# Retention and two feed-forward layers on one core: a planner that models the shared port, and the attention products by single heads

## The chip, the cores and the metric

The kernel runs on 1 core of one Trainium2 chip. The metric is the device time of one execution in microseconds. The engines are named as in the profile: PE (TensorE, matmuls), DVE (VectorE), ACT (ScalarE), POOL (GpSimd) and SP (SyncE, which issues all DMAs here).

## The reference

Inputs q, k, v are 4 batches x 8 heads x 768 positions x 64; two feed-forward layers have w_in 512 x 2048 and w_out 2048 x 512 each.

```python
gamma = 1.0 - 2.0 ** (-5.0 - np.arange(H))
for t in range(S):
    state = gamma * state + np.einsum('bhd,bhe->bhde', k[:, :, t], v[:, :, t])
    y[:, :, t] = scale * np.einsum('bhd,bhde->bhe', q[:, :, t], state)
x = y.transpose(0, 2, 1, 3).reshape(3072, 512)
h = x @ w_in1;  x = (h * np.cos(h)) @ w_out1
h = x @ w_in2;  out = np.where(h > 0, h, exp(min(h, 0)) - 1) @ w_out2
```

## The kernel before

**Retention in units.** The 768 positions are cut into 6 chunks of 128; a chunk of one batch is a unit n (24 units; c = n // 4 is the chunk, b = n % 4 the batch). Heads go in 4 pairs. A unit is loaded as one tile u of 128 x 2048 floats: q and k by features (512 columns each), then v and k by tokens (512 each). Its steps, with the lines of the functions: `load_unit` (430), `scale_unit` (437: q times its decay and scale, v times gamma to the power -(t+1)), `state_unit` (445: the state times gamma to the 128th, written into the two diagonal blocks of a 128 x 128 matrix per pair, as two operations on 64 partitions, whose other blocks a POOL memset at line 896 has zeroed), `scores` (454: 8 matmuls on halves of the rows, then the causal mask by DVE), `values` (474: for c > 0 four 128 x 128 state products, then 8 products of v with the masked scores; ACT and DVE split the result into a high and a low part, x_t) and `update` (505: four 128 x 128 products of k and v, of which the diagonal blocks are added to the state in two operations; none in the last chunk). A matmul of plain float32 shows as two passes in the profile.

**First layer.** Four units make a block of 512 tokens (6 blocks). `hidden` (545) computes a block's hidden units in 8 steps j of 24 matmuls of 512 columns (high and low parts: three products each), and ACT and DVE apply h cos h. The weights come as 64-bit floats and are converted by ACT and three DVE operations each half (lines 322, 325, 329), then split; in block 0 this is `first_weights`, up to 3 steps ahead. Between the hidden products of block i stand the scores, values and updates of the units of block i + 1. The **front** is the attention of units 0 to 3, before the first hidden product. In it `warm` (884) puts matmuls on zeros between the steps; all write one PSUM tile of pool f.

**Later products** use Strassen-Winograd, 7 products of quarter size. `project` (787) is the output product of a layer, on 3 superblocks of 1024 tokens; `hidden2` (638) is the second layer's hidden product, with `seven`, `elu`, `load_x2`, `differences` around it (`product2`, line 630, has its matmuls).

**Order of work.** Every operation is registered with an engine, an estimated time, what it reads and writes, and tiles of pools w 8, hl 4, ld 3, c 11, h 5, eg 3, f 2 (eg and f are PSUM; f has one bank each). `Plan.run` (140) then simulates the engines on the host and so fixes, once, the order of the instructions on each engine. PE keeps the program's order; DVE, ACT, POOL and SP take the ready operation that is due first. An operation marked ANY (scaling, state, differences, part of the preparation of weights) goes to whichever of DVE and POOL takes it first; its two estimates are for DVE and POOL. Where one of them starts an operation between SBUF operands while the other is in one, the estimate of the one that starts is multiplied by CROWDED = 1.6. An operation with an operand in eg or f doesn't count for this.

## Time and profile before

| | us |
|---|---|
| median of 3 runs | 1118.89 (1115.94 to 1121.49) |
| profiled execution | 1118.94 |
| its span | 1117.2 |
| PE / DVE / ACT / POOL busy | 1077.8 / 857.9 / 620.9 / 411.6 |
| front, to the first hidden product | 33.6 |
| first layer's hidden products, to | 378.5 |
| first output product, to | 607 |
| second hidden layer, to | 868.7 |
| second output product, to the end | 1117.2 |

The busy share of an engine is an average over these stages. A stage is read by its own windows, and PE's loss in it is the difference between its length and its matmuls at the pace of a dense stretch. Times in the rows are microseconds from the start of the span; L290 and L295 are the helpers for ACT and for element-wise operations, so such rows are told apart by tiles.

### The profile page before, as it was taken

How to read it: one execution, taken by the hardware profiler on the slowest of the kernel's cores; microseconds unless marked ns; L12 is line 12 of the kernel's file. 1: busy time of each engine (PE TensorE's matmuls, PEld its weight loads, DVE VectorE, ACT ScalarE, POOL GpSimd, SP SyncE). 2: the span in 40 equal slices, each digit the busy share in tenths (PEclk: the TensorE clock that was granted, in tenths of full speed). 3: DMA queues.
4: the chain of work that ended last, by engine and by line, in shares of the span. 5: the costliest groups of instructions: out<-in, count | busy, mean ns of one | idle time of the engine just before them, and what ended most of it. 6: DMA issues, size and time to landing. Idle time of an engine off the chain costs nothing. (4 is left out here: it accounts for less than half of the span.)

```text
span 1117.2 us, 14628 instructions
## 1 busy us (share of the span) xinstructions
PE 1077.8 (96%) x5382; PEld 880.8 (79%) x5384; DVE 857.9 (77%) x884; ACT 620.9 (56%) x719; POOL 411.6 (37%) x300
## 2 busy tenths in 40 slices
PE   7999999999999999999998999999899999999997
PEld 4788888888888888888886787777687788887886
DVE  6998899888899877556649899887798956565452
ACT  3565455554668753443446677767687744443442
POOL 2223462246445734303204874654453421210000
PEclk8999999999999999999999999999899999999999
DMA  8866898988998899999965657877776999998661
GB/s 314 303 226 231 303 332 320 356 295 315 342 345 290 288 347 329 334 334 352 342 246 171 250 215 289 318 287 279 274 259 232 330 343 328 352 347 281 207 207 57
DMA packets 114695, 323.27 MB, mean 289 GB/s; under 512 B 8640, under 2 KB 14912, under 8 KB 112064
## 3 DMA queue, kind: packets, MB, share of 16 engines
q1 hardware_dynamic: 114624, 322.35, 80.9%
q8 instruction: 42, 0.69, 0.2%
q14 instruction: 29, 0.24, 0.1%
HBM read 195.96 MB, written 126.35 MB: 289 GB/s over the span
## 5 line engine op out<-in xcount | busy, mean ns | idle before, releaser
L826 PE MATMUL eg<-hl,w 128*128 128x512 f32 x2016 | 463.7, 390 | 0.0
L295 POOL TENSOR_TENSOR c<-c 128x512 f32<-128x512 f32 (+2 forms) x207 | 305.3, 1486 | 382.6 <-DMA c<-d 138.1
L826 PEld LDWEIGHTS eg<-hl,w 128*128 128x128 f32 x2016 | 376.9, 188 | 77.7
L295 DVE TENSOR_TENSOR hl<-ld,hl 128x1024 fp32r<-128x1024 f32 x168 | 227.7, 1365 | 110.1 <-ACT hl L290 109.7
L290 ACT ACTIVATE hl<-ld 128x1024 fp32r<-128x1024 f32 x168 | 177.9, 1060 | 230.4 <-PE eg L826 219.2
L290 ACT ACTIVATE c<-c 128x1024 f32<-128x1024 f32 (+1 forms) x256 | 231.3, 920 | 79.3 <-DVE c L574 44.3
L557 PE MATMUL eg<-hl,w 128*128 128x512 f32 x1152 | 273.3, 394 | 0.0
L557 PEld LDWEIGHTS eg<-hl,w 128*128 128x128 f32 x1152 | 213.1, 188 | 49.2 <-issue 2.7
L290 ACT ACTIVATE c<-eg 128x1024 int32<-128x1024 f32 (+2 forms) x96 | 87.6, 912 | 98.4 <-PE eg L557 72.9
L630 PE MATMUL eg<-hl,w 128*128 128x512 f32 x432 | 113.3, 398 | 12.5 <-DVE c L295 11.7
L630 PEld LDWEIGHTS eg<-hl,w 128*128 128x128 f32 x432 | 80.4, 190 | 36.1 <-DVE c L295 18.2
L630 PE MATMUL eg<-ld,w 128*128 128x512 f32 x288 | 76.2, 399 | 8.7 <-DVE ld L295 6.5
L295 DVE TENSOR_TENSOR c<-c 128x512 f32<-128x512 f32 (+2 forms) x61 | 49.5, 813 | 31.7 <-DMA c<-d 24.7
L630 PEld LDWEIGHTS eg<-ld,w 128*128 128x128 f32 x288 | 54.9, 191 | 22.3 <-DVE ld L295 7.5
L295 POOL TENSOR_TENSOR ld<-ld,w 128x512 f32<-128x512 f32 x32 | 44.3, 1397 | 72.1 <-DMA ld<-in_attn 58.8
L383 DVE SCALAR_TENSOR_TENSOR w<-c,w 128x768 fp32r<-128x768 f32 (+1 forms) x48 | 65.7, 1383 | 2.8 <-ACT w L290 2.8
L574 DVE SCALAR_TENSOR_TENSOR c<-eg,c 128x1024 f32<-128x1024 f32 x48 | 58.4, 1217 | 9.9 <-ACT c L290 7.3
L579 DVE SCALAR_TENSOR_TENSOR c<-c,eg 128x1024 f32<-128x1024 f32 x48 | 58.4, 1216 | 8.1 <-ACT c L290 7.3
L295 POOL TENSOR_TENSOR h<-c 128x512 f32<-128x512 f32 x22 | 36.4, 1654 | 60.2 <-DMA d<-h 46.5
L290 ACT ACTIVATE w<-c 128x1024 fp32r<-128x1024 f32 (+3 forms) x59 | 52.8, 920 | 9.8 <-DVE c L329 4.1
L329 DVE SCALAR_TENSOR_TENSOR c<-c 128x512 uint32<-128x512 uint32 x64 | 57.0, 900 | 0.7
L325 DVE SCALAR_TENSOR_TENSOR c<-c 128x512 uint32<-128x512 uint32 x64 | 55.1, 872 | 1.0
(50 smaller groups left out, 792.8 us busy)
## 6 DMA issues: line engine op xcount, KB each, us to landing
d<-c SPq DMA_DIRECT2D x205, 512.0 KB, 4.5
ld<-d SPq DMA_DIRECT2D x84, 1024.0 KB, 7.6
c<-d SPq DMA_DIRECT2D x93, 512.0 KB, 6.0
c<-in_weights SPq DMA_DIRECT2D x64, 512.0 KB, 6.7
ld<-in_attn SPq DMA_DIRECT2D x20, 1024.0 KB, 6.5
d<-h SPq DMA_DIRECT2D x32, 256.0 KB, 8.0
out<-c SPq DMA_DIRECT2D x12, 512.0 KB, 4.5
d<-c SPq DMA_DIRECT2D x16, 256.0 KB, 3.1
```

The lines of the kernel that those rows point to most:

```text
L290: plan.op("ACT", us, lambda: nc.scalar.activation(out=out_(), in_=in_(), func=func, **kw), r, w, lag)
L295: e.tensor_tensor(out=out_(), in0=a(), in1=b(), op=op)
L325: plan.op("DVE", 0.69, lambda: nc.vector.scalar_tensor_tensor(out=u(), in0=raw.t[:, :, 1], scalar=0x80000000, in1=u(), op0=ALU.bitwise_and ...
L329: plan.op("DVE", 0.69, lambda: nc.vector.scalar_tensor_tensor(out=u(), in0=raw.t[:, :, 0], scalar=29, in1=u(), op0=ALU.logical_shift_right ...
L383: plan.op("DVE", 0.08 + 0.29 * (hi - lo), lambda: nc.vector.scalar_tensor_tensor(out=w.t[:, lo:hi, 1, :], in0=view(), scalar=turn, in1=hig ...
L557: nc.tensor.matmul(out=h.t[:, half * TB:(half + 1) * TB], lhsT=quarter(j, qd, wpart, kc % 2), rhs=(xh, xl)[xpart].t[:, kc, :], start=(n == ...
L574: plan.op("DVE", 1.22, lambda: nc.vector.scalar_tensor_tensor(out=g.t, in0=h.t, scalar=1.0 / TWO_PI, in1=n(), op0=ALU.mult, op1=ALU.subtra ...
L579: plan.op("DVE", 1.22, lambda: nc.vector.scalar_tensor_tensor(out=g.t, in0=g.t, scalar=1.0, in1=h.t, op0=ALU.subtract, op1=ALU.mult,), [h, ...
L630: nc.tensor.matmul(out=out_(), lhsT=w.t[:, i, wpart, kc * P:(kc + 1) * P], rhs=x.t[:, xpart, kc, :], start=(start and n == 0), stop=(n == ...
L826: nc.tensor.matmul(out=acc.t[:, i * TB:(i + 1) * TB], lhsT=w[:, A_OF[p], wpart, i * P:(i + 1) * P], rhs=hl.t[:, gpart, k, :], start=(p in ...
```

## The change

The planner: the constant CROWDED goes. While DVE and POOL are both in an operation between SBUF operands, both progress at 0.57 of their rate, recomputed at each start and end. POOL starts nothing while DVE is in such an operation.

The attention: state products and updates go head by head, 8 matmuls of 64 x 64 weights, or of 128 x 64 with 64 moving columns, instead of 4; the state is aged in one operation without zero blocks around it, and added or copied in one. The decay of a position is no longer put on v but, for the scores, into a table `fall` of 8 masks that DVE makes at the start, and for the state on k by tokens, in all but the last chunk. `values` needs only q and v of its unit and no longer the whole tile.

The front: unit 3 is loaded into a tile of pool hl instead of ld. Each `warm` has a PSUM tile of its own, given back after it. The last piece of unit 0 (k by tokens) is loaded ahead of unit 1.

```diff
-CROWDED = 1.6
+SHARED = 0.57
...
+        def pace(now):
+            for eng in ("DVE", "POOL"):
+                if eng in doing:
+                    n, left, since, rate, told = doing[eng]
+                    doing[eng] = [n, left - (now - since) * rate, now, rate, told]
+            both = all(e in doing and port[doing[e][0]] for e in ("DVE", "POOL"))
+            for eng in ("DVE", "POOL"):
+                if eng in doing:
+                    d = doing[eng]
+                    d[3] = SHARED if both else 1.0
+                    end = now + max(d[1], 0.0) / d[3]
...
-                if port[n] and busy[other] > now + 0.1 and on_port[other]:
-                    us *= CROWDED
...
+                if eng == "POOL" and "DVE" in doing and port[doing["DVE"][0]] and busy["DVE"] > now + 0.05:
+                    continue
...
     def scale_unit(n, lag=0):
...
         tt("ANY", (0.65, 1.25), q, q, q_tab, ALU.mult, [u[0, 512], tab_at], [u[0, 512]], lag=lag)
-        tt("ANY", (0.65, 1.25), v, v, lambda: v_tab().to_broadcast([P, H, D]), ALU.mult,
-           [u[1024, 1536], tab_at], [u[1024, 1536]], lag=lag)
+        if n // B < UPB - 1:
+            tt("ANY", (0.65, 1.25), k, k, lambda: s_tab().to_broadcast([P, H, D]), ALU.mult,
+               [u[1536, 2048], tab_at], [u[1536, 2048]], lag=lag)
...
-            for j in range(2):
-                r = slice(j * D, (j + 1) * D)
-                tt("ANY", (0.36, 0.75), lambda r=r: diag(n)[r, :, r], lambda r=r: state(b)[r],
+            tt("ANY", (0.36, 0.75), lambda: aged(n), lambda: state(b), lambda: g_tab().to_broadcast([P, NPAIR, D]),
...
-        tt("DVE", 1.23, flat(pt), flat(sc), mask, ALU.mult, [sc, tab_at], [pt], lag=-80)
+        tt("DVE", 1.23, flat(pt), flat(sc), fall, ALU.mult, [sc, fall_at], [pt], lag=-80)
...
-                for a in range(NPAIR):
+            for a in range(NPAIR if c > 0 else 0):
+                for j in range(2):
+                    r = slice(j * D, (j + 1) * D)
                     nc.tensor.matmul(
-                        out=xps.t[:, a, :], lhsT=diag(n)[:, a, :], rhs=q[:, a, :],
+                        out=xps.t[r, a, :], lhsT=aged(n)[r, a, :], rhs=q[r, a, :],
...
-        plan.op("PE", 1.0 if c == 0 else 1.9, go, [u, pt] + ([diag_at(n)] if c > 0 else []), [xps])
+        need = [u[0, 512], u[1024, 1536], pt] + ([aged_at(n)] if c > 0 else [])
+        plan.op("PE", 1.0 if c == 0 else 1.9, go, need, [xps])
...
-                    out=ds.t[:, a, :], lhsT=u.t[:, 1536 + a * P:1536 + (a + 1) * P],
-                    rhs=u.t[:, 1024 + a * P:1024 + (a + 1) * P], start=True, stop=True,
+                        out=ds.t[j * D:(j + 1) * D, a, :], lhsT=u.t[:, 1536 + h0:1536 + h0 + D],
+                        rhs=u.t[:, 1024 + h0:1024 + h0 + D], start=(a == 0), stop=(a == NPAIR - 1),
...
-        plan.op("PE", 1.0, go, [u[1024, 2048]], [ds])
+        plan.op("PE", 0.55, go, [u[1024, 2048]], [ds])
...
-    rest_ps = Buf("f", [P, TB])
-
     def warm(n):
+        rest_ps = Buf("f", [P, TB])
...
     dma(2, lambda: unit0.t[:, 1024:1536], lambda: attn[0, :, 1024:1536], w=[unit0[1024, 1536]])
-    plan.op("POOL", 1.5, lambda: nc.gpsimd.memset(cst.t[:, DIAG:DIAG + 1024], 0.0), [],
-            [cst[DIAG, DIAG + 1024]])
+    dma(2, lambda: unit0.t[:, 1536:2048], lambda: attn[0, :, 1536:2048], w=[unit0[1536, 2048]])
+    tt("DVE", 1.23, lambda: fall().rearrange("p (j a) t -> p j a t", j=2),
...
-    scale_unit(0, "DVE")
+    scale_unit(0)
...
     load_unit(1, EARLY)
-    dma(2, lambda: unit0.t[:, 1536:2048], lambda: attn[0, :, 1536:2048], w=[unit0[1536, 2048]])
...
-    load_unit(3, EARLY)
+    load_unit(3, EARLY, tag="hl")
```

## Rows read from the trace of the kernel before

**Rows 1.** Windows: stretch, length, busy us (instructions) by engine, granted clock, DMA share, GB/s

```profile
6.18:20.00 13.82, 9.42 (x91) 7.37 (x94) 9.28 (x12) 3.86 (x7) 4.88 (x5) 0.83 0.95 344
20.00:33.63 13.63, 10.21 (x99) 7.26 (x96) 12.96 (x17) 7.26 (x14) 3.88 (x4) 0.92 0.91 337
33.63:60.00 26.37, 26.37 (x162) 22.03 (x161) 25.89 (x34) 15.86 (x20) 8.84 (x8) 1.00 0.77 282
60.00:94.50 34.50, 33.83 (x210) 27.87 (x208) 33.84 (x45) 21.92 (x27) 9.24 (x9) 1.00 0.73 247
94.50:330.00 235.50, 235.50 (x1487) 196.45 (x1486) 207.81 (x249) 124.16 (x141) 104.00 (x89) 1.00 0.88 316
...
378.50:607.00 228.50, 228.50 (x1010) 189.27 (x1009) 158.15 (x121) 110.09 (x108) 67.32 (x33) 1.00 0.86 307
607.00:868.70 261.70, 240.46 (x1011) 190.90 (x1010) 225.74 (x248) 188.49 (x250) 147.62 (x105) 0.97 0.74 268
```

The engines stand in the order PE, PE's weight loads, DVE, ACT, POOL.

**Rows 2.** Windows: two openings of superblocks in the second hidden layer

```profile
607.00:627.20 20.20, 15.05 (x56) 11.01 (x54) 18.25 (x13) 13.06 (x16) 15.80 (x10) 0.83 0.93 322
...
779.60:793.50 13.90, 8.38 (x21) 5.59 (x21) 12.35 (x13) 9.18 (x11) 5.55 (x3) 0.63 0.89 308
```

**Rows 3.** Timeline of the front: start, us, engine, line, operation, tiles, count [idle before, releaser]

```profile
13.56 0.68 DVE L295 TENSOR_TENSOR hl<-f,hl 128x512 fp32r<-128x512 f32 x1
...
14.34 1.22 PE L514 MATMUL f<-ld 128*128 128x128 f32 x8 [1.99 <-issue]
...
15.59 1.28 SPq L287 DMA_DIRECT2D ld<-in_attn  x3
...
21.67 0.68 DVE L295 TENSOR_TENSOR hl<-f,hl 128x512 fp32r<-128x512 f32 x1
...
22.45 1.13 PE L514 MATMUL f<-ld 128*128 128x128 f32 x8 [0.57 <-issue]
...
23.66 0.33 SPq L287 DMA_DIRECT2D ld<-in_attn  x1
...
30.84 1.65 POOL L295 TENSOR_TENSOR ld<-ld,w 128x512 f32<-128x512 f32 x1 [4.73 <-DVE c L329]
...
32.54 1.16 PE L464 MATMUL eg<-ld 64*128 64x128 f32 x16 [1.39 <-POOL ld L295]
```

**Rows 4.** Timeline of PE in the dense stretch: L483 state product, L490 v product, L514 update

```profile
39.21 1.05 PE L483 MATMUL f<-ld,w 128*128 128x128 f32 x8
40.19 1.09 PE L490 MATMUL f<-w,ld 128*64 128x128 f32 x16
41.22 5.74 PE L557 MATMUL eg<-hl,w 128*128 128x512 f32 x24
46.80 1.05 PE L514 MATMUL f<-ld 128*128 128x128 f32 x8
47.78 1.16 PE L464 MATMUL eg<-ld 64*128 64x128 f32 x16
48.87 5.73 PE L557 MATMUL eg<-hl,w 128*128 128x512 f32 x24
...
300.49 5.74 PE L557 MATMUL eg<-hl,w 128*128 128x512 f32 x24
306.16 1.16 PE L464 MATMUL eg<-ld 64*128 64x128 f32 x16
```

L557 is the hidden product and L464 the scores; weights stand as rows * columns, then the moving operand.

**Rows 5.** By line: count, shortest/median/longest ns, first and last start

```profile
L329 DVE SCALAR_TENSOR_TENSOR c<-c x64: 676/689/1784, 16.3 to 825.9; 128x512 uint32<-128x512 uint32 x64
...
L574 DVE SCALAR_TENSOR_TENSOR c<-eg,c x48: 1204/1218/1226, 41.5 to 395.0; 128x1024 f32<-128x1024 f32 x48
```

**Rows 6.** Groups of 607 to 868.7 by shape: count, busy us, mean ns, idle before

```profile
L329 DVE SCALAR_TENSOR_TENSOR c<-c 128x512 uint32<-128x512 uint32 x16 | 15.9, 1007 | 0.1
...
L295 POOL TENSOR_TENSOR c<-c 128x512 f32<-128x512 f32 x58 | 90.8, 1566 | 70.6 <-DVE c L740 26.4 <-DVE c L728 24.0 <-issue 14.7
L295 POOL TENSOR_TENSOR c<-c 128x256 f32<-128x256 f32 x45 | 52.8, 1196 | 31.1 <-DMA d<-c 7.8 <-DVE c L728 7.2 <-DVE w L383 6.0
```

More of the change, by code (lines that the diff above doesn't have):

```diff
@@ L155, in run @@
         port = [op[0] in ("DVE", "POOL", "ANY") and not any(b.tag in ("eg", "f") for b in op[4]) for op in ops]
-        on_port = {"DVE": False, "POOL": False}
         def line(n):
@@ L185, in slot_ok @@
             return True
+        doing = {}
+        def pace(now):
[9 more added lines that the diff above has]
+                    end = now + max(d[1], 0.0) / d[3]
+                    if abs(end - d[4]) > 1e-6:
+                        d[4] = busy[eng] = end
+                        heapq.heappush(events, (end, 0, d[0]))
         def start(n, now, eng):
@@ L191, in start @@
             ran_on[n] = eng
-            if eng in on_port:
-                other = "POOL" if eng == "DVE" else "DVE"
-                on_port[eng] = port[n]
-                if port[n] and busy[other] > now + 0.1 and on_port[other]:
-                    us *= CROWDED
             for buf in news:
@@ L201, in start @@
             fn(eng) if ops[n][0] == "ANY" else fn()
-            busy[eng] = now + us
             work[eng] += us
             log.append((now, eng, n))
+            if eng in ("DVE", "POOL"):
+                doing[eng] = [n, us, now, 1.0, 0.0]
+                pace(now)
+                return
+            busy[eng] = now + us
             heapq.heappush(events, (now + us, 0, n))
@@ L220, in run @@
                 eng = ran_on[n]
+                if eng in ("DVE", "POOL"):
+                    if eng not in doing or doing[eng][0] != n or abs(doing[eng][4] - now) > 1e-6:
+                        continue
+                    del doing[eng]
+                    pace(now)
                 done += 1
@@ L245, in run @@
                     continue
-                lines = [ready[eng], flexible] if eng in on_port else [ready[eng]]
+                if eng == "POOL" and "DVE" in doing and port[doing["DVE"][0]] and busy["DVE"] > now + 0.05:
+                    continue
+                lines = [ready[eng], flexible] if eng in ("DVE", "POOL") else [ready[eng]]
                 back = []
@@ L469, in scores @@
         plan.op("PE", 1.0, go, [u[0, 1024]], [sc])
-        mask = lambda: cst.t[:, 512:640].rearrange("p (o t) -> p o t", o=1).to_broadcast([P, H, P])
         flat = lambda x: (lambda: x.t.rearrange("p j a t -> p (j a) t"))
-        tt("DVE", 1.23, flat(pt), flat(sc), mask, ALU.mult, [sc, tab_at], [pt], lag=-80)
+        tt("DVE", 1.23, flat(pt), flat(sc), fall, ALU.mult, [sc, fall_at], [pt], lag=-80)
     def values(n):
@@ L509, in update @@
             return
[L510 removed]
+        ds = Buf("f", [P, NPAIR, D])
         def go():
             for a in range(NPAIR):
[L514 to L526 removed]
+                for j in range(2):
+                    h0 = (2 * a + j) * D
+                    nc.tensor.matmul(
+                        out=ds.t[j * D:(j + 1) * D, a, :], lhsT=u.t[:, 1536 + h0:1536 + h0 + D],
+                        rhs=u.t[:, 1024 + h0:1024 + h0 + D], start=(a == 0), stop=(a == NPAIR - 1),
+                        skip_group_check=True,
+                    )
+        plan.op("PE", 0.55, go, [u[1024, 2048]], [ds])
+        if c == 0:
+            act(0.4, lambda: state(b), lambda: ds.t, [ds], [state_at(b)], lag=-40)
+        else:
+            tt("DVE", 0.42, lambda: state(b), lambda: ds.t, lambda: aged(n), ALU.add,
+               [ds, aged_at(n)], [state_at(b)], lag=-40)
     gd = {(layer, sb): dram_buf([P, NJ, NP, TB]) for layer in range(2) for sb in range(NSB)}
```

44 lines of the change are left out of this document (19 added, 25 removed).

## The prediction

> **What bounds the kernel now.** I read the stages first [rows 1]. TensorE (PE) is busy 235.50 of 235.50 us from 94.5 to 330 and 228.50 of 228.50 in the first output product, where 1010 matmuls take 0.226 us each. No other engine can shorten those stretches; only fewer or shorter PE passes can. Two stretches are different. Before 33.63 us PE idles (9.42 busy of 13.82, then 10.21 of 13.63). And the second hidden layer, 607 to 868.7, takes 261.70 us for 1011 matmuls that are worth 1011 x 0.226 = 228.7, so it loses 33.0. In [rows 2] 7.5 of these are lost at 607 to 627.2 (20.20 less 56 x 0.226) and 9.2 at 779.6 to 793.5 (13.90 less 21 x 0.226), where a new superblock's inputs are split and the granted clock falls to 0.83 and 0.63 after PE has waited; the other 16.3 are spread.
>
> The third reading is VectorE (DVE) between the front and the end of block 0. It is idle 4.54 us of 6.18 to 20, but only 1.81 us of the 74.5 after that (12.96 + 25.89 + 33.84 busy) [rows 1]. So PE looks dense there while DVE, which converts the weights of block 0, has no room either. Whatever the front gains must pass this gate.
>
> In the timeline of the front [rows 3] the reader is to see PE waiting for a PSUM bank of the pool f: update(0) starts at 14.34, right after DVE's split of x at 13.56 for 0.68 us has ended, and update(1) at 22.45, after the split at 21.67. One of the two f banks is held by the clock-keeping matmuls, so values and update take turns on the other. Unit 3 is asked for at 15.59, when update(0) has freed unit 0's slot, and unit 4 at 23.66, after update(1). Its scaling ends at 30.84 + 1.65, and PE has its first scores at 32.54 after a wait of 1.39.
>
> **The change part by part.** The sum is made against the profiled execution, 1118.94 us (span 1117.2 and 1.7 around it); the median of the runs shown is 1118.89, so nothing is shifted.
>
> Front: f bank, unit 3 in hl, k of unit 0 earlier. update(0) no longer waits 1.99, update(1) 0.57, the first scores 1.39 [rows 3]; the matmuls between them also run at a granted 0.83 and 0.92 [rows 1], so I put PE's possible gain at 4 (those waits) to 8 us. The DVE gate caps it: DVE can take back at most its 4.54 us of idle time, plus the work that leaves it up to the end of block 0. That is one state addition of 0.42 us (the planner's own cost, in the code) per unit instead of two: four units, 1.7 us. Less some 0.6, because the new product of mask and decay (1.23 in the code) stands where unit 0's v was scaled (0.65). So the cap is 4.54 + 1.1 = 5.6. Not every gap can be filled: I take **-4.0**, ends 0 and -5.6. What the moves cost: unit 0's k goes past the three loads of unit 1 on SP, 0.26 MB at 344 GB/s [rows 1], 0.8 us later for unit 1, of which the cap leaves room. New waits: the mask waits for the new table, computed on the same engine ahead of it; update waits for k to be scaled, and behind update on PE the next scores are queued, but between scaling and update lies a whole hidden product of 5.6 us after the front. The POOL memset that goes and the ACT copies of state (8 to 4) lie beside other work: 0, and nothing if that cover is gone, as removed work cannot delay.
>
> State products by heads, in the dense stretch. A block's length is the distance of starts in [rows 4]. The old state product takes 39.21 to 40.19 = 0.98, the old update 46.80 to 47.78 = 0.98, each 8 passes with 128 weight rows, columns and moving columns. The product of v and scores, 16 passes on two column halves with 128 moving columns, takes 1.03; the scores, 16 passes on two row halves, 1.09. The hidden product before a tiled block lasts 5.67 (300.49 to 306.16) where one before a full block lasts 5.58 (41.22 to 46.80): changing over costs 0.09. The new state product has 16 passes on two diagonal quarters with 128 moving columns. No row shows a quarter. Bounds: 1.03 + 0.09 = 1.12 if it goes like the two halves, and 0.52 + 0.09 = 0.61 if smaller weights halve it. The scores have twice the weight columns of the v product and take about as long (1.09 and 1.03), so the moving columns seem to set the pace and these stay: I take 1.12, +0.14. The new update has 64 moving columns, 16 passes. Bounds again 0.61 and 1.12; since the moving columns halve I take half of 1.03 without about 0.15 for starting and ending, 0.15 again, and 0.09, which is 0.68: -0.30. In block 0 the DVE gate rules, so 16 of the 20 state products and 12 of the 20 updates count (four updates lie in the front): 16 x 0.14 - 12 x 0.30 = **-1.4**, ends 28 x 0.14 = +3.9 and 28 x -0.37 = -10.4.
>
> The rows give a block 0.064 us per pass whatever its shape on halves (1.03 over 16) [rows 4], so the number of passes could be the limit instead of the columns; then the update costs 1.12 and PE gains nothing. The Trainium skill, page "TensorE: Matmul & The Clock Gate", section "Wait — 56ns, not 53.3ns?", gives such a rule: with hardware decode off the sequencer spends about 62 ns on each MATMUL. By it the update would take 16 x 0.062 = 0.99, no gain over 0.98; the trace does not contradict it here.
>
> Decay in the mask: v is no longer scaled, k is, with the same shape and as many instructions until the last four units, which drop one each; on POOL these are off the path: 0. One state_unit operation on 128 partitions replaces two on 64; POOL's time, 0.
>
> Port-aware planner. It alters no work, only the order per engine and which of DVE and POOL takes the free operations. Nothing in the trace of before shows the new order, so this is the widest term. What the rows show: a DVE operation with an operand in PSUM is never delayed (L574: 1204 to 1226 ns over 48), one between SBUF operands can be (L329: median 689, up to 1784) [rows 5]. In the second hidden layer the 16 of L329 average 1007, so 0.32 us above the median each, while POOL's 58 operations of 512 columns average 1566 [rows 6]. The old planner counted 1.25 for these and stretched only the later of two that meet; the new one slows both and lets POOL begin when DVE is off the port. An order made from truer lengths should have fewer late arrivals among the 16.3 us spread over this stage, and may do better or worse at the two openings. I take **-3**, about a fifth of 16.3; ends -16 (all spread waits gone) and +12 (the slower rival below). In the output products PE is dense and DVE has 70 us free [rows 1]: there a new order costs 0.
>
> The rows also speak against the planner's model. The longest L329, 1784, is one of 689 plus about 1.1, as if it stood still until a POOL operation had ended, and not run at half speed. The Trainium skill says so: page "SBUF — State Buffer", section "Who interferes with whom": the pair of ports that both engines share is an exclusive lock held for a whole instruction, and the loser waits. By that, a POOL operation that starts in the shadow of a PSUM operation of 0.68 still blocks the next DVE operation, and the planner term would be 0.
>
> Sum: 1118.94 - 4.0 - 1.4 - 3 = 1110.5.
>
> **The rivals.**
> A, given back: the front's gain is eaten at the DVE gate (units 4 to 7 wait for weights), a tile pair costs its 1.12, and the new order is worth nothing: -0.5 to +3.9, about 1119. For it: DVE's 1.81 idle us in 74.5 [rows 1]. Against: 4.54 idle us before them.
> B, slower: DVE takes the free operations that POOL may not begin. In the second hidden layer DVE is busy 225.74 of 261.70 and PE needs 228.7 [rows 1]: DVE has 3 us to spare. An operation of 512 columns moved to DVE adds 0.69 and saves a meeting worth 0.32, net some 0.3 over both sizes. From 10 moved operations on this lengthens the stage. Half of the 103 [rows 6] moved, 52, gives (52 - 10) x 0.3 = 12.6, so 1118.94 - 5.4 + 12.6 = 1126. For it: DVE looks for work at every end, POOL only off the port. Against: three or four PSUM operations a step give POOL its openings.
> C, more: the openings at 607 and 779.6 close too, as their loads and splits come in time: 13 of 16.7 us more, 1097. For it: in both DVE and POOL work side by side. Against: the loads at the openings have little to do with the port.
> That the lock and not the sharing holds is the forecast without the planner's 3: 1113.5, inside the forecast's own spread.
>
> **How the numbers follow.** Forecast (1103 to 1114.5) 0.45, A (1114.5 to 1122) 0.20, B (above 1122) 0.15, C (below 1103) 0.20. Leaving out B and the lower part of C (0.05) gives the range 1095 to 1122, which holds 0.8; it takes in the bounds of the PE term (-10.4, +3.9) around the rest. Half a per cent, 5.6 us, is about what a measurement of this kernel can tell from no change: below 1113.3 lie C and nearly all of the forecast, 0.62; above 1124.5 most of B, 0.13; between them 0.25.
>
> **What would show it.** In the front: update(0) near 12.4 without a wait, unit 3 asked for before 10 us, the first hidden product at 26 to 30 instead of 33.63, and then the gate: PE waits for weights in 45 to 90 and the end of block 0 only about 4 us earlier. Blocks: update 0.6 to 0.75, state product 1.0 to 1.15; 0.5 for both would make the dense stretch 10 us shorter. Second hidden layer: PE's loss below 33, L329's mean below 1007, POOL's count not far under 105. I am wrong if POOL's count halves and DVE is above 230 us there (B), if block 0 ends where it did (A), or if the openings' 16.7 us vanish (C).

## The result, and the profile after

The changed kernel took 1108.38 us in the median (1105.53 to 1110.73, 5 runs); the kernel before took 1117.52 in the runs beside it. The ratio is 0.9916, interval 0.9901 to 0.9931: faster by 0.84%. The forecast was 1110.5, range 1095 to 1122. The profiled execution of the changed kernel took 1108.38 us with a span of 1106.6.

Lines moved: helpers are L314 (ACT) and L319 (element-wise) now, L491 scores, L510 state product, L517 v product, L544 update, L586 first hidden product, L659 second, L855 output products, L353 what L329 was. The kernels of the experiments have line numbers of their own; there rows are told apart by their tiles. First the windows of the changed kernel, cut where the first matmul of each product starts; block 0 ends one matmul (0.23) after the start of its last hidden matmul, and the last output product is counted to the start of its last matmul. The columns are those of [rows 1].

```profile
6.38:26.14 19.76, 15.24 (x220) 11.43 (x221) 16.79 (x22) 7.15 (x13) 8.34 (x7) 1.00 1.02 370
26.14:87.03 60.89, 59.29 (x418) 46.72 (x416) 57.82 (x79) 38.66 (x48) 13.24 (x11) 1.00 0.82 296
87.03:370.36 283.33, 283.33 (x1938) 227.75 (x1938) 237.17 (x288) 165.22 (x185) 95.72 (x85) 1.00 0.87 312
370.36:598.84 228.48, 228.48 (x1010) 189.19 (x1009) 156.00 (x147) 109.25 (x107) 19.76 (x11) 1.00 0.88 311
598.84:857.14 258.30, 239.53 (x1009) 191.23 (x1008) 219.90 (x275) 188.42 (x250) 104.20 (x76) 0.98 0.74 271
857.14:1099.20 242.06, 239.51 (x1096) 197.39 (x1095) 142.87 (x135) 107.19 (x110) 9.61 (x7) 1.00 0.79 276
```

Cut in the same way, from the trace of one execution each (us; the stages of every kernel that was run). Two executions of one order came out 1.5 apart at the end of block 0 (e12, below).

| kernel | front | block 0 | its end | rest of first layer | output product 1 | hidden 2 | output product 2 |
|---|---|---|---|---|---|---|---|
| before | 33.63 | 60.05 | 93.7 | 284.90 | 228.48 | 261.47 | 241.24 |
| changed | 26.14 | 60.89 | 87.0 | 283.33 | 228.48 | 258.31 | 242.06 |
| e1 planner only | 29.60 | 61.69 | 91.3 | 284.59 | 228.48 | 258.66 | 243.25 |
| e2 without planner | 25.18 | 60.81 | 86.0 | 283.33 | 231.89 | 260.82 | 241.64 |
| e3 without front | 29.91 | 60.79 | 90.7 | 283.33 | 228.48 | 258.52 | 243.73 |
| e4 without heads | 28.55 | 63.62 | 92.2 | 284.59 | 228.48 | 259.22 | 241.05 |
| e5 front only | 26.02 | 63.81 | 89.8 | 284.75 | 228.48 | 261.02 | 244.82 |
| e6 without bank | 28.27 | 61.62 | 89.9 | 284.79 | 228.59 | 258.30 | 239.61 |
| e7 waiting in the planner | 26.28 | 61.07 | 87.4 | 293.79 | 232.33 | 256.77 | 244.15 |
| e9 state steps split | 25.16 | 67.60 | 92.8 | 283.33 | 229.02 | 260.86 | 240.46 |
| e10 without hold | 25.17 | 61.94 | 87.1 | 290.23 | 228.48 | 269.05 | 240.61 |
| e11 unit 3 in ld | 26.82 | 60.53 | 87.3 | 283.33 | 228.48 | 258.29 | 239.01 |
| e12 mixed planner | 25.40 | 62.08 | 87.5 | 283.33 | 228.48 | 257.29 | 243.11 |

From before to changed the span fell by 10.6 us: 6.7 to the end of block 0, 1.6 in the rest of the first layer, 3.2 in the second hidden layer, and 0.8 back in the last output product. That last column lies between 239.0 and 244.8, and no part of the change was found that explains it.

The front of the changed kernel, in its timeline, answers to [rows 3]: update(0) starts at 13.13 after an idle 0.57, unit 3 is asked for from 7.58 on and update(1) follows the clock-keeping group without a wait. TensorE's granted clock is another part of it: in the trace of before it stands at the lower of its two levels, 0.50 (1.2 GHz instead of 2.4), from 15.30 to 22.00, after PE had waited 1.99, and the v product there lasts 1.98 instead of 1.09. The blocks of that stretch took some 2.4 us more than the same ones at full clock. In the changed kernel's front the clock is 1.00 throughout.

Before (a window), then the changed kernel (timeline):

```profile
15.30:22.00 6.70, 5.64 (x37) 3.65 (x35) 4.89 (x7) 2.59 (x5) 2.83 (x3) 0.50 0.81 272
```

```profile
7.58 0.33 SPq L311 DMA_DIRECT2D hl<-in_attn  x1
...
13.13 0.69 PE L544 MATMUL f<-ld 128*64 128x64 f32 x16 [0.57 <-issue]
...
17.31 0.69 PE L544 MATMUL f<-ld 128*64 128x64 f32 x16
...
23.00 0.69 PE L544 MATMUL f<-ld 128*64 128x64 f32 x16 [1.60 <-DVE ld L319]
```

The blocks of the dense stretch (timeline of PE) answer to [rows 4]. The state product is 290.27 to 291.29, 1.02, after a hidden product of 5.67; the update 40.35 to 40.96, 0.61, after one of 5.67.

```profile
34.68 5.74 PE L586 MATMUL eg<-hl,w 128*128 128x512 f32 x24
40.35 0.69 PE L544 MATMUL f<-ld 128*64 128x64 f32 x16
40.96 1.16 PE L491 MATMUL eg<-ld 64*128 64x128 f32 x16
...
284.60 5.74 PE L586 MATMUL eg<-hl,w 128*128 128x512 f32 x24
290.27 1.09 PE L510 MATMUL f<-ld,w 64*64 64x128 f32 x16
291.29 1.09 PE L517 MATMUL f<-w,ld 128*64 128x128 f32 x16
```

In the second hidden layer (groups by shape of the changed kernel) POOL has 42 + 33 + 1 operations instead of the 58 + 45 + 2 of before, and the operation between SBUF operands that averaged 1007 ns [rows 6] averages 881:

```profile
L353 DVE SCALAR_TENSOR_TENSOR c<-c 128x512 uint32<-128x512 uint32 x16 | 13.9, 881 | 0.2
...
L319 POOL TENSOR_TENSOR c<-c 128x512 f32<-128x512 f32 x42 | 64.3, 1530 | 95.2 <-DVE c L757 43.8 <-DVE c L769 24.2 <-issue 9.1
L319 POOL TENSOR_TENSOR c<-c 128x256 f32<-128x256 f32 x33 | 36.6, 1128 | 54.4 <-DVE c L319 30.4 <-DMA d<-c 7.5 <-ACT c L314 7.2
```

### The profile page after: what moved, and what is told of

Read it like the earlier page. It is cut to its first block, busy times and chain, and to the rows that moved or that the text cites. A ratio compares the mean times of both kernels' runs of the same rounds, so it can differ in the third digit from the quotient of the medians.

```text
span 1106.6 us, 15144 instructions
## 1 busy us (share of the span) xinstructions
PE 1071.6 (97%) x5704; PEld 866.1 (78%) x5704; DVE 831.5 (75%) x944; ACT 619.0 (56%) x715; POOL 251.1 (23%) x200
## 5 line engine op out<-in xcount | busy, mean ns | idle before, releaser
L855 PE MATMUL eg<-hl,w 128*128 128x512 f32 x2016 | 463.7, 390 | 0.0
L855 PEld LDWEIGHTS eg<-hl,w 128*128 128x128 f32 x2016 | 376.8, 188 | 77.8
L314 ACT ACTIVATE hl<-ld 128x1024 fp32r<-128x1024 f32 x168 | 178.1, 1061 | 237.7 <-PE eg L855 234.5
L319 DVE TENSOR_TENSOR hl<-ld,hl 128x1024 fp32r<-128x1024 f32 x168 | 216.6, 1295 | 109.3 <-ACT hl L314 109.0
L319 POOL TENSOR_TENSOR c<-c 128x512 f32<-128x512 f32 (+2 forms) x137 | 182.1, 1338 | 443.6 <-DMA c<-d 81.3
L586 PE MATMUL eg<-hl,w 128*128 128x512 f32 x1152 | 273.9, 394 | 1.6 <-DVE w L319 0.7
L314 ACT ACTIVATE c<-c 128x1024 f32<-128x1024 f32 (+1 forms) x256 | 231.4, 920 | 58.7 <-DVE c L603 33.3
L586 PEld LDWEIGHTS eg<-hl,w 128*128 128x128 f32 x1152 | 213.0, 188 | 51.5 <-issue 3.4
L314 ACT ACTIVATE c<-eg 128x1024 int32<-128x1024 f32 (+2 forms) x96 | 87.4, 910 | 92.7 <-PE eg L586 73.0
L659 PE MATMUL eg<-hl,w 128*128 128x512 f32 x432 | 113.9, 400 | 10.6 <-DVE c L319 10.5
L319 DVE TENSOR_TENSOR c<-c 128x512 f32<-128x512 f32 (+2 forms) x131 | 89.5, 695 | 36.6 <-DMA c<-d 34.4
L659 PEld LDWEIGHTS eg<-hl,w 128*128 128x128 f32 x432 | 81.7, 192 | 33.3 <-DVE c L319 11.4
L659 PE MATMUL eg<-ld,w 128*128 128x512 f32 x288 | 76.4, 400 | 6.5 <-DVE ld L319 5.2
L659 PEld LDWEIGHTS eg<-ld,w 128*128 128x128 f32 x288 | 55.0, 192 | 20.1 <-DVE ld L319 6.2
L319 POOL TENSOR_TENSOR ld<-ld,w 128x512 f32<-128x512 f32 x29 | 38.1, 1322 | 108.6 <-DMA ld<-in_attn 108.6
L314 ACT ACTIVATE w<-c 128x1024 fp32r<-128x1024 f32 (+3 forms) x59 | 53.0, 920 | 10.2 <-DVE c L353 6.7
L407 DVE SCALAR_TENSOR_TENSOR w<-c,w 128x768 fp32r<-128x768 f32 (+1 forms) x48 | 56.1, 1185 | 2.0 <-ACT w L314 2.0
L349 DVE SCALAR_TENSOR_TENSOR c<-c 128x512 uint32<-128x512 uint32 x64 | 48.9, 779 | 0.8
L353 DVE SCALAR_TENSOR_TENSOR c<-c 128x512 uint32<-128x512 uint32 x64 | 49.1, 785 | 0.3
L319 DVE TENSOR_TENSOR c<-eg,h 128x512 f32<-128x512 f32 x48 | 32.9, 686 | 20.2 <-PE eg L659 18.3
```

Of the source, the lines that this page charges most:

```text
L314: plan.op("ACT", us, lambda: nc.scalar.activation(out=out_(), in_=in_(), func=func, **kw), r, w, lag)
L319: e.tensor_tensor(out=out_(), in0=a(), in1=b(), op=op)
L349: plan.op("DVE", 0.69, lambda: nc.vector.scalar_tensor_tensor(out=u(), in0=raw.t[:, :, 1], scalar=0x80000000, in1=u(), op0=ALU.bitwise_and ...
L353: plan.op("DVE", 0.69, lambda: nc.vector.scalar_tensor_tensor(out=u(), in0=raw.t[:, :, 0], scalar=29, in1=u(), op0=ALU.logical_shift_right ...
L407: plan.op("DVE", 0.08 + 0.29 * (hi - lo), lambda: nc.vector.scalar_tensor_tensor(out=w.t[:, lo:hi, 1, :], in0=view(), scalar=turn, in1=hig ...
L586: nc.tensor.matmul(out=h.t[:, half * TB:(half + 1) * TB], lhsT=quarter(j, qd, wpart, kc % 2), rhs=(xh, xl)[xpart].t[:, kc, :], start=(n == ...
```

## The experiments

**The three parts apart.** My first theory was the one of the prediction: a gate of DVE in block 0 that caps the front's gain, products worth what their blocks say, and a planner worth 3 us in the second hidden layer.

e1 puts the new planner into the kernel before:

```diff
-CROWDED = 1.6
+SHARED = 0.57
...
+            both = all(e in doing and port[doing[e][0]] for e in ("DVE", "POOL"))
...
+                    d[3] = SHARED if both else 1.0
...
-                if port[n] and busy[other] > now + 0.1 and on_port[other]:
-                    us *= CROWDED
...
+                if eng == "POOL" and "DVE" in doing and port[doing["DVE"][0]] and busy["DVE"] > now + 0.05:
+                    continue
```

> The kernel before with the new planner alone. Theory: the planner is worth the 3 us that the second hidden layer lost less (261.5 to 258.3 us from its first to its last matmul), and frees DVE in block 0, which without a shorter front shows as nothing: 1114 to 1116 us, first hidden product within 1 us of 33.6. Rival 1, the order of that stage comes out by luck with each list of operations: anything from 1110 to 1125, second hidden layer 255 to 270. Rival 2, the planner moves the front too, as it alone gives the free scalings to the engines differently: first hidden product before 31 us.

Measured 1116.27, ratio 0.9990 (0.9975 to 1.0004): no difference to be told. The second hidden layer came to 258.7, as expected, and the front to 29.6, which the theory did not have (rival 2); block 0 was 1.6 longer and the last output product 2.0, and they took half of it back. Of the 4.0 us in the front some 2.4 are the stretch at the lower clock, which e1's front does not have. Whether the new order keeps it away or this one execution was spared it was not tested.

e2 puts the old planner into the changed kernel, the same edit backwards:

```diff
-SHARED = 0.57
+CROWDED = 1.6
...
-                if eng == "POOL" and "DVE" in doing and port[doing["DVE"][0]] and busy["DVE"] > now + 0.05:
-                    continue
```

> The changed kernel with the old planner (CROWDED 1.6, POOL may always begin). Theory, the DVE gate: the first hidden product is still at about 26 us, but PE waits for weights until the end of block 0, which comes no earlier than 89 us (87.1 in the changed kernel, 93.7 before), and the second hidden layer is at 261 to 262 again: 1111 to 1114 us. Rival, no gate: the end of block 0 stays at 87 to 88, and the whole is at most 3 us over the changed kernel, 1109 to 1112, all of it in the second hidden layer.

Measured 1112.11, ratio 0.9948 (0.9928 to 0.9968). The theory falls on block 0: its end came at 86.0, not at 89 or later. So the gate as I had drawn it was not there, even with the old planner. The second hidden layer was at 260.8, close to what the theory had, and 3.4 us were lost where nobody expected them, in the first output product. Its timeline:

```profile
508.35 7.01 DVE L295 TENSOR_TENSOR hl<-ld,hl 128x1024 fp32r<-128x1024 f32 x4
...
508.63 3.37 POOL L295 TENSOR_TENSOR c<-c 128x1024 f32<-128x1024 f32 x1
...
509.81 3.02 PE L831 MATMUL eg<-hl,w 128*128 128x512 f32 x12 [1.39 <-DVE hl L295]
```

POOL is in one operation of 3.37 us, DVE's splits beside it stretch, and PE waits 1.39 for them in a stage where DVE has 70 us free. With two later waits for DVE (0.32 and 0.81) this makes 2.5 of the 3.4 us.

e3 takes the front back out of the changed kernel:

```diff
-    def warm(n):
-        rest_ps = Buf("f", [P, TB])
+    rest_ps = Buf("f", [P, TB])
+    def warm(n):
...
-    load_unit(3, EARLY, tag="hl")
+    load_unit(3, EARLY)
```

> The changed kernel with one PSUM tile for all clock-keeping matmuls and unit 3 in the pool ld again (unit 0's k stays early). Theory: the front is 7 us longer, the first hidden product at 32 to 34, and all of it stays to the end: 1114 to 1116 us. Rival, the gate after all: the PE waits of block 0 vanish with the later start and only 4 us are lost: 1111 to 1113.

Measured 1111.76, ratio 0.9943 (0.9923 to 0.9963). The front was 29.9, not 32 to 34: half of the 7.5 us is there without the bank and unit 3. Some 2.4 of it are the lower clock of before, which e3's front does not have either; what unit 0's early k, the lighter steps and the planner share of the rest was not separated. What the bank and unit 3 give, 3.8 us, stays to the end of block 0 (90.7 against 87.0), and block 0 is as long (60.8 and 60.9): the theory on its place was right, its size was not.

e4 keeps the new planner and front and takes the old products, with decay on v:

```diff
-    nc.tensor.matmul(out=xps.t[r, a, :], lhsT=aged(n)[r, a, :], rhs=q[r, a, :], ...)
+    nc.tensor.matmul(out=xps.t[:, a, :], lhsT=diag(n)[:, a, :], rhs=q[:, a, :], ...)
...
-        if n // B < UPB - 1:
-            tt("ANY", (0.65, 1.25), k, k, lambda: s_tab().to_broadcast([P, H, D]), ALU.mult, ...)
+        tt("ANY", (0.65, 1.25), v, v, lambda: v_tab().to_broadcast([P, H, D]), ALU.mult, ...)
```

> The changed kernel with the state products and updates of before (four 128 x 128 products each, decay on v, two aging operations, the zeroed blocks), but the new planner and the new front. Theory, from the blocks measured in the changed kernel (update 0.62 + 0.09 for 0.98, state product 1.02 + 0.09 for 0.98): PE needs 16 x 0.28 - 20 x 0.13 = 1.9 us more, so 1109.5 to 1111 us. Rival 1, the aging in one operation and the shorter additions on DVE count too: 1112 to 1115. Rival 2, nothing of it is seen behind the order of the later stages: within 1 us of the changed kernel or below it.

Measured 1113.39, ratio 0.9961 (0.9944 to 0.9977): rival 1. Of the 6.3 us between the two profiled spans (1112.9 and 1106.6), 1.3 are in the rest of the first layer, which is what the PE blocks give; the larger part, 5.1 us, lies before the end of block 0, in the front (28.6) and in PE waits for DVE. So the products' largest effect is not in PE's own blocks.

**The gate, second attempt.** If the new products take work from DVE, the cap should hold with the old ones. e5 is the kernel before with the new front alone:

```diff
-    rest_ps = Buf("f", [P, TB])
     def warm(n):
+        rest_ps = Buf("f", [P, TB])
...
+    dma(2, lambda: unit0.t[:, 1536:2048], lambda: attn[0, :, 1536:2048], w=[unit0[1536, 2048]])
...
     load_unit(1, EARLY)
-    dma(2, lambda: unit0.t[:, 1536:2048], lambda: attn[0, :, 1536:2048], w=[unit0[1536, 2048]])
...
-    load_unit(3, EARLY)
+    load_unit(3, EARLY, tag="hl")
```

> The kernel before with the new front alone (a PSUM tile for each clock-keeping group, unit 3 in hl, unit 0's k early), old planner, old products. The gate of DVE in block 0, second attempt: the cap was wrong for the changed kernel because the new products and the decay in the mask take work from DVE; with the old ones the cap holds. Then the first hidden product comes at 27 to 29.5 us, PE waits 1.5 us or more for DVE in block 0, its end comes at 91 to 92.5 (93.7 before), and the whole gains 1 to 3 us: 1115 to 1117. Rival, there is no gate with the old products either: the stretch from the first hidden product to the end of block 0 stays 60 us, its end comes at 87 to 89.5 and the whole gains 4 to 6 us: 1112 to 1114.

Measured 1115.48, ratio 0.9977 (0.9961 to 0.9992). The front was 26.0, 7.6 shorter; block 0 lasted 63.8 instead of 60.1, so 3.9 us were left at its end, close to the 4.0 of the prediction. It ended at 89.8, earlier than the 91 expected here and at the edge of the rival; the PE waits (two of the five of 0.3 us or more are shown) speak for the gate.

```profile
57.70 1.16 PE L514 MATMUL f<-ld 128*128 128x128 f32 x8 [1.31 <-DVE w L295]
...
61.22 5.30 PE L557 MATMUL eg<-hl,w 128*128 128x512 f32 x22 [0.60 <-DVE w L295]
```

The windows of block 0 show whether DVE had room: kernel before, e5 and e4 (old products), then e2 (new products); the changed kernel's is above.

```profile
33.63:93.69 60.06, 59.39 (x362) 49.09 (x361) 59.23 (x77) 37.17 (x45) 18.08 (x16) 1.00 0.75 261
```

```profile
26.02:89.82 63.80, 60.23 (x362) 48.77 (x361) 62.85 (x84) 40.78 (x52) 17.46 (x16) 1.00 0.74 267
```

```profile
28.55:92.16 63.61, 60.14 (x360) 48.93 (x361) 62.31 (x84) 40.18 (x51) 16.02 (x14) 1.00 0.71 253
```

```profile
25.18:85.98 60.80, 59.40 (x418) 46.59 (x416) 57.84 (x77) 39.27 (x49) 19.77 (x13) 1.00 0.83 303
```

With the old products DVE is idle 0.83, 0.95 and 1.30 us of the block, whatever the front; with the new ones 2.96 and, in the changed kernel, 3.07. The table says the same of all kernels: with the old products block 0 grows as the front shrinks (60.1 after a front of 33.6, 61.7 after 29.6, 63.6 after 28.6, 63.8 after 26.0), with the new ones it lasts 60.5 to 62.1 after fronts of 25.2 to 29.9, in all but e9. The gate is there with the old products and open with the new.

What DVE is spared shows when its busy time is summed up to the end of block 0: 80.25 us in e5, 75.24 in e2, which has the same planner and front (windows, then the conversion steps by line, e5 and e2 in turn):

```profile
0.00:89.82 89.82, 81.41 (x558) 63.28 (x561) 80.25 (x107) 50.20 (x68) 26.16 (x28) 1.00 0.80 292
...
0.00:85.98 85.98, 79.90 (x648) 59.67 (x648) 75.24 (x100) 47.87 (x63) 27.73 (x23) 1.00 0.86 313
```

```profile
L325 DVE SCALAR_TENSOR_TENSOR c<-c 128x512 uint32<-128x512 uint32 x18 | 12.5, 729 | 0.0
L322 DVE TENSOR_SCALAR c<-c 128x512 uint32<-128x512 uint32 x18 | 9.1, 531 | 0.6 <-ACT c L290 0.6
...
L325 DVE SCALAR_TENSOR_TENSOR c<-c 128x512 uint32<-128x512 uint32 x16 | 10.8, 695 | 0.1
L322 DVE TENSOR_SCALAR c<-c 128x512 uint32<-128x512 uint32 x16 | 6.6, 435 | 0.1
```

State additions and agings on DVE are only 1.7 us less and the new table costs 1.2. The 5.0 lie in the conversion and splitting of weights, 46.9 us in e5 and 41.9 in e2: two half conversions are not taken ahead of time (2.2 us), and the operations last less long (2.8).

e9 asks which part of them opens it. On e2 it ages, adds and copies the state in two operations on 64 partitions again:

```diff
-            tt("ANY", (0.36, 0.75), lambda: aged(n), lambda: state(b), ...)
+            for j in range(2):
+                r = slice(j * D, (j + 1) * D)
+                tt("ANY", (0.36, 0.75), lambda r=r: aged(n)[r], lambda r=r: state(b)[r], ...)
...
-            tt("DVE", 0.42, lambda: state(b), lambda: ds.t, lambda: aged(n), ALU.add, ...)
+            for j in range(2):
+                tt("DVE", 0.42, lambda r=r: state(b)[r], lambda r=r: ds.t[r], lambda r=r: aged(n)[r], ALU.add, ...)
```

> The changed kernel with the old planner (as the run without the planner) and, besides, the state aged and added or copied in two operations on 64 partitions again; the products by heads and the decay in the mask stay. Theory, the room of DVE in block 0 comes from the state steps, the additions on DVE and POOL's agings that hold the port: the end of block 0 moves from 86.0 to 88 us or later, most of the way to the 89.8 of the new front on the old products. Rival, it comes from the rest (the decay in the mask, the shorter PE blocks, fewer conversions taken ahead of time): the end of block 0 stays within 1 us of 86.0.

Measured 1114.23, ratio 0.9964 (0.9945 to 0.9982), against 1112.11 of e2. Block 0 lasted 67.6 instead of 60.8, more than the theory asked. Part of that is what one PE wait starts: after 2.34 us of waiting for DVE the following matmuls run in a stretch with a mean granted clock of 0.76, partly at the lower level (0.50 from 38 to 41; timeline of PE, then the window).

```profile
36.96 6.91 PE L567 MATMUL eg<-hl,w 128*128 128x512 f32 x22 [2.34 <-DVE w L295]
```

```profile
36.90:43.90 7.00, 6.94 (x24) 5.29 (x26) 6.34 (x9) 4.21 (x5) 0.00 (x0) 0.76 0.61 222
```

The conversions take 47.6 us up to the end of block 0, as much as with the old products, though the products by heads stay. So splitting the state steps is enough to lose what the new products gave; how much of the 6.8 us is their time and how much the order that the planner made around them was not separated. The order has a part in it: the end at 92.8 lies 3.0 behind e5's, where all of the products are old, and DVE is idle 2.39 us of the block here.

**What in the front.** e6 is the changed kernel with one PSUM tile for all clock-keeping matmuls (the first hunk of e3), e11 with unit 3 in ld (its second).

> The changed kernel with one PSUM tile for all clock-keeping matmuls; unit 3 still in hl. Theory, the bank carries the front: update and values take turns on one bank again, the first hidden product at 29 to 30 us as without both, 1111 to 1112.5. Rival, the load of unit 3 carries it: at 26 to 27.5, within 1.5 us of the changed kernel.

> The changed kernel with unit 3 in the pool ld again; each clock-keeping group still has its own PSUM tile. The run without the bank gave a first hidden product at 28.3 against 26.1, the run without both 29.9. If the two add, this one is at 27.5 to 28.3; rival, either is enough to lose most: 28.5 to 30. Whole 1108 to 1111.

e6: 1110.42, ratio 0.9934 (0.9918 to 0.9950), front 28.3, between the two answers, end of block 0 at 89.9. e11: 1107.88, ratio 0.9897 (0.9875 to 0.9919), front 26.8, below what either answer asked, and end of block 0 at 87.3. Of the 3.8 us that both give in the front (e3), the bank alone accounts for 2.1 and unit 3 alone for 0.7. Most of the 2.1 is clock: after a PE wait of 1.67 e6 runs from 20.40 to 23.60 at the lower level, 0.50, with PE busy all the time, 1.6 us lost. Of the whole, moving unit 3 gives nothing that can be told: the intervals of e11 and of the changed kernel overlap.

**The port.** e8 measures it by itself, without any part of the computation.

```diff
+        dve(16);  pool(512, 8)
+        dve(10);  pool(2048, 2)
+        dve_ps(10);  pool(2048, 2)
```

> No part of the computation, a measurement of the port: DVE and POOL subtract SBUF tiles, first DVE alone (6 of 128x512), then POOL alone (6 of 512), then side by side (16 of DVE against 8 of POOL), then 10 of DVE against 2 POOL operations of 2048 columns, and last 10 of DVE with one operand in PSUM against 2 of 2048. The output is zeros. Theory, waiting: against the long POOL operations one or two DVE operations last 4 us or more, as long as POOL's rest, and the others 0.7; side by side in turns, DVE up to 1.8. Rival, sharing at about 0.57: every DVE operation under a POOL operation lasts about 1.2 us, whatever the length of POOL's. In both the operations with PSUM stay at 0.7.

The timeline, DVE's operation of 512 columns beside POOL's of 2048, and then by line (shortest, median, longest) DVE between SBUF tiles and with one operand in PSUM:

```profile
50.04 4.49 POOL L45 TENSOR_TENSOR pc<-pa,pb 128x2048 f32<-128x2048 f32 x1
50.07 5.01 DVE L37 TENSOR_TENSOR dc<-da,db 128x512 f32<-128x512 f32 x1
...
54.61 4.82 POOL L45 TENSOR_TENSOR pc<-pa,pb 128x2048 f32<-128x2048 f32 x1
55.11 4.87 DVE L37 TENSOR_TENSOR dc<-da,db 128x512 f32<-128x512 f32 x1
```

```profile
L37 DVE TENSOR_TENSOR dc<-da,db x32: 691/693/5007, 16.5 to 64.4; 128x512 f32<-128x512 f32 x32
...
L41 DVE TENSOR_TENSOR dc<-ps,db x10: 691/691/691, 65.4 to 71.9; 128x512 f32<-128x512 f32 x10
```

An operation of 0.69 us lasts 5.01 when it starts 0.03 us after a POOL operation of 4.49: it waits for the whole of it. Then POOL's next lasts 4.82 instead of 4.49, which fits a wait for the rest of DVE's. The PSUM operand makes DVE free of it, 691 ns ten times out of ten. This is waiting, not sharing, as the Trainium skill has it (page "SBUF — State Buffer", section "Who interferes with whom"); the new planner's 0.57 for both describes something that the chip does not do.

e7 therefore gives the planner a waiting rule:

```diff
+                if port[n] and other in doing and port[doing[other][0]]:
+                    us += max(0.0, busy[other] - now)
...
-            both = all(e in doing and port[doing[e][0]] for e in ("DVE", "POOL"))
+            both = False
```

> The changed kernel with another model in the planner: an operation between SBUF operands that starts while the other engine is in one waits until that one has ended and then runs at full speed, instead of both running at 0.57; the rule that POOL begins only off DVE's port stays. Theory, waiting is what the chip does: a truer plan, second hidden layer 250 to 257 us (258.3 in the changed kernel), whole 1101 to 1107. Rival, the order is as good as it gets with either model: 1107 to 1111; or by luck worse, up to 1115.

Measured 1121.57, ratio 1.0029 (1.0013 to 1.0044): slower than the kernel before, and worse than the worst that was expected. The second hidden layer was the shortest of all with 256.8, but the rest of the first layer took 293.8 instead of 283.3, and the first output product 232.3 instead of 228.5. In the first layer two PE waits for DVE, 3.15 and 2.80, were each followed by a stretch at the lower level of the clock (timeline of PE, then the window around the first, with 0.50 from 129 to 135):

```profile
129.29 1.98 PE L520 MATMUL f<-w,ld 128*64 128x128 f32 x16 [3.15 <-DVE w L322]
```

```profile
126.00:134.00 8.00, 4.85 (x27) 3.81 (x24) 7.72 (x10) 3.51 (x5) 2.55 (x2) 0.66 0.47 153
```

e10 leaves the rate of 0.57 and drops the other rule of the planner:

```diff
-                if eng == "POOL" and "DVE" in doing and port[doing["DVE"][0]] and busy["DVE"] > now + 0.05:
-                    continue
```

> The changed kernel without the rule that POOL begins only while DVE is off the port; the rate of 0.57 for both stays. Theory, the rule carries the planner's gain, since it takes operations off POOL (76 instead of 105 in the second hidden layer): without it that stage is at 260.5 to 262 us and POOL has 95 to 110 operations there; whole 1110 to 1113. Rival, the truer rate carries it: the stage stays at 258 to 259, whole 1107 to 1110.

Measured 1125.70, ratio 1.0062 (1.0041 to 1.0083): 17 us over the changed kernel, far over either answer. POOL has 98 operations in the second hidden layer again (windows, first line), and DVE is busy 232.65 us there, more than before the change:

```profile
605.82:874.87 269.05, 241.22 (x1010) 193.70 (x1009) 232.65 (x262) 190.50 (x252) 137.27 (x98) 0.95 0.75 272
148.00:158.00 10.00, 6.33 (x43) 5.37 (x44) 9.15 (x13) 3.48 (x4) 6.92 (x6) 0.66 0.94 360
```

The rate alone does harm: 269.1 us in that stage where the planner of before, with neither, has 260.8 (e2). With the rule the stage takes 258.3, or 256.8 with e7's price. So the rule is what the shorter stages have in common, whatever the price; the rule with the old price of 1.6 was not run. The second window is the place in the first layer where PE waited 3.98 for DVE; the mean granted clock there is 0.66, and 0.50 from 150 to 156.

```profile
151.67 1.12 PE L542 MATMUL f<-ld 128*64 128x64 f32 x16 [3.98 <-DVE hl L317]
```

e12 tries to keep the better of both planners, the old model up to the first output product and the new one after it:

```diff
     assert not converts
+    plan.turn = len(plan.ops)
...
+                late = pe_at >= len(pe) or pe[pe_at] >= self.turn
-                if eng == "POOL" and "DVE" in doing and port[doing["DVE"][0]] and busy["DVE"] > now + 0.05:
+                if late and eng == "POOL" and "DVE" in doing and port[doing["DVE"][0]] and busy["DVE"] > now + 0.05:
...
-                    d[3] = SHARED if both else 1.0
+                    d[3] = SHARED if both and min(doing["DVE"][0], doing["POOL"][0]) >= self.turn else 1.0
...
+                if n < self.turn and port[n] and other in doing and port[doing[other][0]] and busy[other] > now + 0.1:
+                    us *= CROWDED
```

> The changed kernel with the old model of the planner for the first layer's attention and hidden products and the new one from the first output product on. The old model had block 0 end at 86.0 instead of 87.0 but lost 3.4 us in the first output product and 2.5 in the second hidden layer; the mix should keep the better of each: first hidden product at 25.2, end of block 0 at 86.0, output product 228.5, second hidden layer 258 to 259, whole 1105.5 to 1108. Rival, the last output product, 239.6 to 244.8 us over the runs so far, hides the 1 us: anything from 1104 to 1111.

Measured 1108.36, ratio 0.9901 (0.9882 to 0.9920): the same as the changed kernel. The first output product kept its 228.5 and the second hidden layer came to 257.3, but block 0 ended at 87.5 where e2 had 86.0. On DVE and on POOL its instructions stand in the same order as e2's up to 357 us, so 1.5 us between two executions of one order is scatter. Differences of that size in the table's block 0 column are not to be read, the planner's 1.0 among them.

No version beats the changed kernel by more than the measurement can tell.

## Why the prediction was right or wrong

**The whole** was right, 1108.38 for 1110.5, with one term too small by 2.7 us and one right by luck.

**Front, -4.0: mis-sized, measured 7.5 at the first hidden product and 6.7 at the end of block 0.** The PE side, 4 to 8 us from the waits of [rows 3] and the lower clock, was right: 7.6 in e5. (The front of e1, with the new planner alone, is 4.0 shorter; the two do not add, and the stretch at the lower clock, gone in both, counts once.) The gate was real when the front comes alone: e5 gains 7.6 and keeps 3.9, within DVE's 4.54 idle us. That this is also the -4.0 of the sum is chance, since e5 has none of the 1.1 that the sum counts for the state steps. The term that was mis-sized is this 1.1, the work that leaves DVE up to the end of block 0, and with it the 0 for the agings on POOL. Measured: DVE's busy time up to there is 5.0 us less with the new products (80.25 in e5, 75.24 in e2; 76.63 in e12, the same order once more), and the end comes 3.8 us earlier (89.8 and 86.0; 2.3 with e12's 87.5). The state steps themselves leave DVE no more than the sum says; the rest is conversions that last less long or are not taken ahead. Up to that point DVE's own additions halve, and POOL's agings are four in the changed kernel where they were ten before; e8 shows that such an operation can stop DVE for its length, and e9, where they are split again, has the conversions back at 47.6 us. How much comes from the agings and how much from the order was not measured. What is off the path on POOL is not free when DVE is the gate. I had also counted idle time as the whole of DVE's room: before the change it had by then taken two half conversions of later weights (18 of L325 against 16), which could have waited.

**PE blocks, -1.4: right, measured -1.6** (rest of the first layer, 284.90 to 283.33; 283.33 in six of the kernels with the new products; 284.59 in e1 and e4, so 1.3 are the blocks and 0.3 is not explained). State product 1.02 + 0.09 for the 1.12 taken, update 0.61 + 0.09 for 0.68. The moving columns set the pace: with the same weights of 128 x 64 and the same 16 passes, 64 of them take 0.61 where 128 take 1.02 (v product, L517). The rule weighed against it, about 62 ns for each MATMUL with hardware decode off (the Trainium skill, page "TensorE: Matmul & The Clock Gate", section "Wait — 56ns, not 53.3ns?"), did not bind here: 0.61 over 16 is 38 ns. The rival from the rows, 0.064 us a pass whatever its shape, fails by the same number.

**Planner, -3: right in size, -3.2, by luck.** I argued that truer lengths give an order with fewer late arrivals among the spread waits, and that the openings would do better or worse by chance. It came out the other way round: the spread waits stayed and one opening shrank. The stage has the same 1008 products in the same order in all kernels, so its loss (time less 0.2262 for each matmul, 228.48 over 1010) can be told by place: the first 60 matmuls, and 24 from the 337th and from the 673rd on, are the three openings of superblocks.

| loss in the second hidden layer | opening 1 | opening 2 | opening 3 | spread | all |
|---|---|---|---|---|---|
| before | 9.5 | 2.6 | 9.4 | 12.0 | 33.5 |
| changed | 9.3 | 4.5 | 4.8 | 11.7 | 30.3 |
| e7 waiting in the planner | 7.3 | 8.5 | 7.6 | 5.4 | 28.8 |
| e10 without hold | 10.2 | 7.0 | 7.2 | 16.5 | 40.8 |

The gain is what the third opening wins less what the second loses (windows of the three, before and changed):

```profile
607.07:630.13 23.06, 16.85 (x62) 12.21 (x60) 21.11 (x17) 15.29 (x19) 18.66 (x13) 0.85 0.88 308
694.93:702.91 7.98, 6.08 (x25) 4.35 (x24) 7.98 (x10) 6.17 (x8) 5.69 (x3) 1.00 0.78 268
778.73:793.61 14.88, 9.36 (x26) 6.41 (x25) 13.33 (x14) 9.96 (x12) 5.55 (x3) 0.66 0.84 291
```

```profile
598.84:621.70 22.86, 15.69 (x61) 11.71 (x60) 20.28 (x20) 16.47 (x21) 13.77 (x8) 0.96 0.92 327
686.84:696.75 9.91, 7.63 (x26) 5.57 (x24) 8.25 (x9) 7.71 (x10) 5.03 (x4) 0.83 0.95 342
772.01:782.23 10.22, 7.57 (x25) 5.63 (x24) 7.10 (x8) 7.68 (x10) 3.50 (x4) 0.83 0.94 335
```

At the third DVE has 8 operations where it had 14, PE idles 2.65 us instead of 5.52, and less of the stretch runs at the lower clock (0.83 for 0.66). The stage took 258.3 to 259.2 in the six kernels with the whole new planner, 257.3 in e12, and 260.8 to 261.5 in the four with the old one. That is less than it seems: in this stage DVE and POOL have one and the same order in the first seven and another in the last four, so two orders were compared, and that of the new planner may be a lucky one. The argument itself did better in e7, the price nearest to what e8 shows: its spread waits fell to 5.4; but its openings take 23.4 where those of the changed kernel take 18.6, and it lost 10.5 us in the rest of the first layer and 3.9 in the first output product. For the whole kernel the planner is worth 3.7 us by the medians with the new products (e2) and nothing that can be told with the old (e1).

**Rival B** happened in its mechanism and failed in its price. 29 of POOL's operations went to DVE there (105 to 76), beyond the 10 from which it was to decide, but DVE's busy time fell from 225.74 to 219.90. I had taken 0.69 paid for 0.32 saved; the saving must be larger. One POOL operation can stop DVE for its whole length (e8); what each of the 29 saved was not measured.

**Output products, 0.** Right for this order (228.48 before and after), but not because DVE has room there: e2 lost 3.4 us in that stage, 2.5 of them in PE waits for DVE, and e7 3.9. And the last output product moved by 0.8, within what it does from one order to the next.

**Rival A** is e5 in its first half: the gate does take back half of the front's gain, if the products stay as they were. **Rival C** had the openings at 607 and 779.6 close: the first stayed (9.5 to 9.3), the other halved (9.4 to 4.8), which is 4.8 of its 13 us.

## What to carry to other kernels

Where DVE is what an otherwise dense stretch waits for, count POOL's operations between SBUF operands as possible DVE time, each up to its full length; an edit that looks idle on POOL may be the one that lets another edit's gain through. Try such edits together and apart, because the gain of one can stand or fall with the other. With an order made by a simulation, a truer price for the meeting of two engines did not make a better kernel here: it shortened one stage and lengthened two others (e7). Before calling a gain the planner's, count how many different orders stand behind it: seven kernels with one order are one case.

## What the runs showed of the hardware

A DVE operation of 0.69 us stood still for the whole of a POOL operation of 4.49 us and lasted 5.01; ten with an operand in PSUM, beside POOL operations of the same size, kept their 0.69 (e8). A pass of 128 x 64 weights with 64 moving columns, two column halves in turn, takes 38 ns (0.61 over 16). A single PE wait cost more than itself, as matmuls after it ran at the lower of the clock's two levels, 1.2 GHz instead of 2.4: after 2.34 us of waiting 22 matmuls and a change of shape took 6.84 instead of 5.22 (e9), after 3.15 a v product and a hidden product 9.51 instead of 6.69 (e7).
